# The gated unit's two products as 2x2 blocks: seven block products for eight

## The chip, the cores and the metric

The kernel runs on one core of a Trainium2 chip. The time is the device time of one execution in microseconds (us). TensorE multiplies matrices, VectorE and ScalarE work element by element and may read and write PSUM, GpSimd works on SBUF only, SyncE issues transfers.

## The reference

A linear attention feeds a router with eight experts (all float32), and its result x (1536 tokens, 384 features) a gated unit. The change concerns the last function:

```python
def _moe2_ref(x, w_gate, w_val, w_out) -> np.ndarray:
    g = x @ w_gate
    silu = g * (1.0 / (1.0 + np.exp(-g)))
    val = x @ w_val
    return (silu * val @ w_out).astype(np.float32)
```

w_gate and w_val are 384 x 1536, w_out is 1536 x 384, all three given as float64.

## The kernel before

The stages follow one another: attention and routing, experts, gated unit. A number is split in a high half (a rounded copy, made by ScalarE) and a low half (the rest, by VectorE or GpSimd: "lowered"), and each product is three matmuls: high x high, high x low, low x high.

**Gated unit.** The 1536 hidden features are six chunks c of 256, each two f of 128; the 384 input features are three k blocks of 128; the tokens are four groups g of 384 (TG). For a chunk and a group, `inner` sums gate and value over k in two PSUM banks for each f, 36 matmuls of 384 columns in all; ScalarE takes the Silu (L1095), VectorE multiplies (L1096), ScalarE rounds (L1099), GpSimd lowers (L1100). `outer` multiplies by w_out, three tiles of 128 tokens a group (L1111 to L1113, six matmuls a tile and chunk), and adds to `acc` (L1118 for the first chunk, L1120 later). Chunks 0 to 2 run chunk by chunk. For chunks 3 to 5 the group is the outer loop, and a tile sums all three chunks in PSUM; then it is stored by an indirect DMA from GpSimd's queue (L1122).

**Conversion.** `convert_all` turns the float64 weights into halves: 18 items (gate, value and output weights of each chunk), 768 columns each. An item's steps: Square on ScalarE and L811 on VectorE; L817; L823; L830 (all VectorE); the high half (ScalarE, L837); the low half (L842, on VectorE during the experts and on GpSimd in the gated unit). A new item starts every five calls of `background`, which stand by hand between the other work. 15 calls stand in the experts stage; chunks 0 and 1 have buffers there (`mp`), a third buffer comes with the gated unit.

**Experts.** Eight experts of 16 steps f (eight up, eight down). Each expert's own weights are split by ScalarE (L732) and VectorE (L733). The last expert also splits the tokens of groups 0 and 1 (`x2_split`).

On every engine the order of the code is the order of work. PSUM has eight banks: three for `pa_tile`, and in the gated unit two for `pg2` and three for `ps_o`.

Of the kernel before, what the change touches and what calls it, by code (L numbers as in the profile page):

```python
# [23 lines left out]
P = 128  # L24
# [36 lines left out]
FF_WEIGHTS = {"w_gate": [P, KD, 256], "w_val": [P, KD, 256], "w_out": [P, 2, DM]}  # L61
# [8 lines left out]
class Kernel:  # L70
# [14 lines left out]
    def run(self):  # L85
        tc, nc = self.tc, self.nc
        with ExitStack() as top, tc.manual_schedule():
# [7 lines left out]
            with ExitStack() as ex:  # L95
# [9 lines left out]
                self.x2s = [[mp.tile([P, KD, TG], F32R, name=f"x2{q}{g}") for q in "hl"] for g in range(2)]  # L105
                self.wff = [self.weights_ff(mp, i) for i in range(2)]
# [656 lines left out]
    def convert_all(self):  # L763

        items = [(m, c) for c in range(NC) for m in FF_WEIGHTS]

        def load(i):
            if i < len(items):
                m, c = items[i]
                raw = self.mp.tile([P, 2 * UC], I32, name="raw64", tag="raw64", bufs=2)  # L770
                self.nc.sync.dma_start(out=raw, in_=self.a[m][c].bitcast(I32))
                return raw, self.convert(lambda: self.wff[c % 3][m])
# [3 lines left out]
        for n in range(5 * len(items) + 1):  # L776
            if n % 5 == 0:
                cur[n // 5 + 1] = load(n // 5 + 1)
            for i in (n // 5 - 1, n // 5):
                j = n - 5 * i  # L780
                if 0 <= i < len(items) and j < 6:
                    raw, steps = cur[i]
                    steps[j](raw)
# [10 lines left out]
    def weights_ff(self, pool, i):  # L794

        return {
            m: [pool.tile(shape, F32R, name=f"{m}_{q}{i}") for q in ("hi", "lo")] for m, shape in FF_WEIGHTS.items()
        }

    def convert(self, outs):  # L800
# [4 lines left out]
        word = lambda raw, i: raw.rearrange("p (c two) -> p c two", two=2)[:, :, i]  # L805

        def s0(raw):
            t["mag"] = self.mp.tile([P, cols], F32, name="mag", tag="mag", bufs=2)
            nc.scalar.activation(t["mag"], word(raw, 1).bitcast(F32), AF.Square)
            t["bits"] = self.mp.tile([P, cols], I32, name="bits", tag="bits", bufs=2)  # L810
# [17 lines left out]
        def s3(raw):  # L828
# [3 lines left out]
            )  # L832

        def s4(raw):
            hi_out = outs()[0]
            t["m3"] = t["mag"].rearrange("p (a b) -> p a b", a=hi_out.shape[1])
            nc.scalar.copy(hi_out, t["m3"])  # L837

        def s5(raw):
            hi_out, lo_out = outs()  # L840

            (nc.vector if self.in_experts else nc.gpsimd).tensor_sub(lo_out, t["m3"], hi_out.bitcast(F32))  # L842

        return [s0, s1, s2, s3, s4, s5]


# [101 lines left out]
    def experts(self, st):  # L948
# [53 lines left out]
        last, xrs = None, {}  # L1002
        for e in range(E):
            hc, py = self.tiles()
            for f in range(2 * NF):
# [8 lines left out]
                if f == (5 if e == 0 else 1):  # L1014
# [8 lines left out]
                    if e == 0:  # L1023
                        self.background(1, 2)
# [13 lines left out]
                if f in ((12, 14) if 0 < e < E - 3 else (10, 12, 14) if 0 < e < E - 1 else ()):  # L1038
                    self.background(1, 2)
# [6 lines left out]
                if e == E - 1 and NF <= f < NF + 2 * KD:  # L1046
                    self.x2_split((f - NF) // KD, [(f - NF) % KD])
# [8 lines left out]
    def x2_split(self, g, ks):  # L1056
        nc = self.nc
        xh, xl = self.x2s[g]
        src = self.x2[:, :, g * TG:(g + 1) * TG]
        for k in ks:  # L1060
            nc.scalar.copy(xh[:, k], src[:, k])
            nc.vector.tensor_sub(xl[:, k], src[:, k], xh[:, k].bitcast(F32))

    def gated(self, st, at_end=lambda: None):
        nc, a = self.nc, self.a
        NG, NTT = N // TG, TG // P
        wk = self.pool(st, "wk", side="right")
        pg2 = self.pool(st, "pg2", 2, space=PSUM)
        ps_o = self.pool(st, "ps_o", 3, space=PSUM)
        self.wff.append(self.weights_ff(wk, 2))  # L1070
        self.x2s += [[wk.tile([P, KD, TG], F32R, name=f"x2{q}{g}") for q in "hl"] for g in range(2, NG)]
# [3 lines left out]
        acc = wk.tile([P, NT, DM], F32, name="acc")  # L1075
        later = []

        def inner(c, g, steps, limit):

            parts = []  # L1080
            xh, xl = self.x2s[g]
            for f in range(2):
                pg = {}
                if later:
                    self.x2_split(*later.pop(0))
                fs = slice(f * P, (f + 1) * P)
                for m in ("w_gate", "w_val"):
                    wh, wl = self.wff[c % 3][m]
                    pg[m] = (pg2.tile([P, 512], F32, name="g2", tag="g2") if f else self.pa_tile())[:, 0:TG]
                    for k in range(KD):  # L1090
                        nc.tensor.matmul(pg[m], lhsT=wh[:, k, fs], rhs=xh[:, k], start=(k == 0), stop=False)
                        nc.tensor.matmul(pg[m], lhsT=wh[:, k, fs], rhs=xl[:, k], start=False, stop=False)
                        nc.tensor.matmul(pg[m], lhsT=wl[:, k, fs], rhs=xh[:, k], start=False, stop=(k == KD - 1))  # L1093
                sg = wk.tile([P, TG], F32, name="sg", tag="sg", bufs=3)
                nc.scalar.activation(sg, pg["w_gate"], AF.Silu)  # L1095
                nc.vector.tensor_mul(sg, pg["w_val"], sg)  # L1096
                h_ = wk.tile([P, TG], F32R, name="ah", tag="ah", bufs=8)
                l_ = wk.tile([P, TG], F32R, name="al", tag="al", bufs=8)
                nc.scalar.copy(h_, sg)  # L1099
                nc.gpsimd.tensor_sub(l_, sg, h_.bitcast(F32))  # L1100
                parts.append((h_, l_))
                self.background(steps, *limit)
            return [(c, f, *parts[f]) for f in range(2)]
# [194 lines left out]
```

## Time and profile before

| | us |
|---|---|
| three runs | 442.28, 443.30, 443.99 (median 443.3) |
| profiled execution | 444.58 |
| its span, first to last instruction | 442.9 |
| TensorE, matmuls | 428.2 busy, 97% |
| VectorE | 288.1 busy, 65% |
| ScalarE | 213.4 busy, 48% |
| GpSimd | 155.8 busy, 35% |

The span is counted from the first to the last instruction of the profiled execution; the time includes what lies around it. In profile rows PE is TensorE's matmuls, PEld its weight loads, DVE VectorE, ACT ScalarE, POOL GpSimd.

### The profile page before, as it was taken

The numbers are of one execution on the slowest core, as the hardware profiler recorded it, in microseconds if no ns is written. First come the engines' busy times: TensorE is split into PE (matmuls) and PEld (weight loads), VectorE is DVE, ScalarE is ACT, GpSimd is POOL, SyncE is SP. The second block draws the span as 40 slices with busy tenths as digits, with TensorE's granted clock in tenths as the row PEclk, the third lists the DMA queues.
The fourth block names the chain that finished last, engine by engine and source line by source line (L and its number), as shares of the span: only waits on it lengthen the run. The fifth ranks groups of instructions, "written<-read, shape, count | busy, mean of one in ns | idle before, by whom it ended". The sixth has DMA issues, their size and how long they took to land. (4 is left out here: it accounts for less than half of the span.)

```text
span 442.9 us, 8350 instructions
## 1 busy us (share of the span) xinstructions
PE 428.2 (97%) x3180; PEld 415.7 (94%) x3180; DVE 288.1 (65%) x559; ACT 213.4 (48%) x470; POOL 155.8 (35%) x147
## 2 busy tenths in 40 slices
PE   8889999999999999999999999999999999999991
PEld 7778889999999999999999999999999999999991
DVE  6979996867887888895685879988774121212120
ACT  2677784656666666665465533444252121220310
POOL 5845653101120110000444546463565323232331
PEclk9989999999999999999999999999999999999997
DMA  7998952699999999602023242324200100001001
GB/s 259 356 304 274 360 226 89 195 362 304 347 222 219 294 253 228 230 1 73 0 80 122 86 142 73 123 92 142 74 0 1 53 1 22 32 0 56 1 21 41
DMA packets 24817, 63.78 MB, mean 144 GB/s; under 512 B 4800, under 2 KB 10048, under 8 KB 24768
## 3 DMA queue, kind: packets, MB, share of 16 engines
q1 hardware_dynamic: 22128, 57.43, 41.7%
q0 software_dynamic: 1920, 4.73, 2.9%
q10 hardware_dynamic: 720, 1.00, 0.8%
q8 instruction: 27, 0.44, 0.4%
q14 instruction: 22, 0.18, 0.1%
HBM read 55.67 MB, written 7.48 MB: 143 GB/s over the span
## 5 line engine op out<-in xcount | busy, mean ns | idle before, releaser
L1100 POOL TENSOR_TENSOR al<-sg,ah 128x384 fp32r<-128x384 f32 x48 | 54.5, 1135 | 128.2 <-ACT ah L1099 128.2
L733 DVE TENSOR_TENSOR wlo<-raw,whi 128x768 fp32r<-128x768 f32 x60 | 57.3, 956 | 9.7 <-ACT whi L732 8.8
L1099 ACT CAST ah<-sg 128x384 fp32r<-128x384 f32 x48 | 24.7, 515 | 78.0 <-DVE sg L1096 78.0
L865 PE MATMUL py<-hc,whi 128*128 128x448 f32 x192 | 62.2, 378 | 0.0
L876 PE MATMUL A<-xc,whi 128*128 128x224 f32 x336 | 56.7, 274 | 0.0
L866 PE MATMUL py<-hc,wlo 128*128 128x224 f32 x192 | 51.4, 268 | 0.0
L876 PEld LDWEIGHTS A<-xc,whi 128*128 128x128 f32 x336 | 51.0, 192 | 0.1
L732 ACT CAST whi<-raw 128x768 fp32r<-128x768 f32 x60 | 49.8, 837 | 1.3 <-PE py L865 0.7
L1111 PE MATMUL po<-w_out_hi,ah 128*128 128x384 f32 x144 | 48.6, 337 | 0.0
L1113 PE MATMUL po<-w_out_hi,al 128*128 128x384 f32 x144 | 48.5, 337 | 0.0
L1112 PE MATMUL po<-w_out_lo,ah 128*128 128x384 f32 x144 | 48.5, 337 | 0.0
L876 PE MATMUL A<-xc,wlo 128*128 128x224 f32 x168 | 46.1, 275 | 0.0
L943 POOL DMA_INDIRECT ids<-tok,by_expert x12 | 13.6, 1133 | 79.0 <-DMA ids<-tok,by_expert 71.1
L1120 DVE TENSOR_TENSOR acc<-acc,po 128x384 f32<-128x384 f32 x36 | 19.3, 546 | 30.9 <-PE po L1113 30.9
L865 PEld LDWEIGHTS py<-hc,whi 128*128 128x128 f32 x192 | 36.3, 189 | 2.7
L866 PEld LDWEIGHTS py<-hc,wlo 128*128 128x128 f32 x192 | 36.7, 191 | 0.0
L1096 DVE TENSOR_TENSOR sg<-g,sg 128x384 f32<-128x384 f32 x24 | 13.3, 555 | 35.8 <-PE g L1093 31.1
L1096 DVE TENSOR_TENSOR sg<-A,sg 128x384 f32<-128x384 f32 x24 | 13.3, 554 | 35.5 <-PE A L1093 31.8
L895 ACT ACTIVATE hc<-A 128x224 fp32r<-128x224 f32 x64 | 23.2, 362 | 21.2 <-PE A L876 18.4
L278 ACT ACTIVATE AT<-ident,c 128x128 f32<-128x128 f32 x96 | 29.4, 389 | 8.2 <-DVE c L265 8.2
L876 PEld LDWEIGHTS A<-xc,wlo 128*128 128x128 f32 x168 | 32.3, 192 | 0.0
L1095 ACT ACTIVATE sg<-A 128x384 f32<-128x384 f32 x24 | 11.7, 486 | 34.1 <-PE A L1093 34.1
(177 smaller groups left out, 1096.9 us busy)
## 6 DMA issues: line engine op xcount, KB each, us to landing
raw<-in_w SPq DMA_DIRECT2D x62, 384.0 KB, 7.6
rkT<-in_rkT SPq DMA_DIRECT2D x12, 512.0 KB, 5.6
rk<-in_rk SPq DMA_DIRECT2D x12, 384.0 KB, 5.6
raw<-in_w_gate SPq DMA_DIRECT2D x6, 768.0 KB, 4.2
raw<-in_w_val SPq DMA_DIRECT2D x6, 768.0 KB, 4.4
raw<-in_w_out SPq DMA_DIRECT2D x6, 768.0 KB, 4.5
x_disp<-zero SPq DMA_DIRECT2D x8, 336.0 KB, 7.6
xr<-x_disp SPq DMA_DIRECT2D x8, 336.0 KB, 6.5
```

The costliest lines, as they stand in the source:

```text
L278: nc.scalar.activation(AT[i][:, j, hp], ident, AF.Copy, scale=cc[i][:, j, hp:hp + 1])
L732: nc.scalar.copy(h_, raw)
L733: nc.vector.tensor_sub(l_, raw, h_.bitcast(F32))
L865: nc.tensor.matmul(ps[:, 0:2 * BLK], lhsT=wh, rhs=xc, start=first, stop=False, skip_group_check=True)
L866: nc.tensor.matmul(ps[:, HI], lhsT=wl, rhs=xc[:, HI], start=False, stop=last, skip_group_check=True)
L876: self.nc.tensor.matmul(ph[:, HI], lhsT=w[:, k, fs], rhs=x[1][:, k, half], start=(k == 0 and i == 0), stop=(k == KD - 1 and i == 2),)
L1096: nc.vector.tensor_mul(sg, pg["w_val"], sg)
L1099: nc.scalar.copy(h_, sg)
L1100: nc.gpsimd.tensor_sub(l_, sg, h_.bitcast(F32))
L1111: nc.tensor.matmul(po, lhsT=ah[:, ts_], rhs=wh, start=(i == 0), stop=False)
L1112: nc.tensor.matmul(po, lhsT=ah[:, ts_], rhs=wl, start=False, stop=False)
L1113: nc.tensor.matmul(po, lhsT=al[:, ts_], rhs=wh, start=False, stop=(i == len(parts) - 1))
```

## The change

Two groups of tokens make a pair p, x1 and x2. Over the k blocks 0 and 1, [gate; value] times [x1, x2] is a 2x2 by 2x2 block product, and seven products take the place of eight, at the price of sums: four of weights (S1 to S4, two VectorE operations in each of the value's steps s4 and s5, then a high and a low half of 1024 columns), four of tokens (T1 to T4, in `x_pair`: four steps for each pair, eight in all), and some of results. The k block 2 keeps its four plain products. A `block` is a chunk, a pair and one f.

Banks are now `pb` (from `pa_tile`), and `pa`, `pc`, `pd` of their own: `pb` collects gate x x11, is copied to `pa` by ScalarE, goes on to collect; `pc` and `pd` are written by VectorE as `pb + m5`, and products are added on top of all three. Two matmuls at the start open the banks that are written by other engines. `ps_o` has two banks.

The output tiles (`sum_tile`, six matmuls) stand between the products; all six chunks are now added into `acc` by VectorE (the first is copied by ScalarE as before). The weights have two buffers, and only chunk 0's in the experts stage; 19 calls of `background` stand there instead of 15, always three in experts 1 to 6. In a block three to six calls are placed (four in the steady chunks, none in the first two blocks, which run the token sums of pair 1). The Silu table is loaded in the last expert. The value of `gate0` is multiplied at the end of a block, and its halves are taken at the start of the next.

```diff
+GATE, VAL1, VAL2, S1, S2, S3, S4 = 0, 3, 4, 5, 6, 7, 8
+X11, X21, X31, X22, X32, T1, T2, T3, T4 = range(9)
+NW, NX = 9, 9
...
-                self.x2s = [[mp.tile([P, KD, TG], F32R, name=f"x2{q}{g}") for q in "hl"] for g in range(2)]
-                self.wff = [self.weights_ff(mp, i) for i in range(2)]
+                self.xb = [self.x_rooms(mp, 0)]
+                self.wff = [self.weights_ff(mp, 0)]
...
+        shapes = {"in": [P, NW, 256], "out": [P, 2, DM]}
+        return {m: [pool.tile(shape, F32R, name=f"w{m}_{q}{i}") for q in ("hi", "lo")] for m, shape in shapes.items()}
...
+            self.gate_m3 = t
+            return [s0, s1, s2, s3, lambda raw: high(t["m3"], GATE, KD), lambda raw: low(t["m3"], GATE, KD)]
...
+            high(t["m3"][:, 1:3], VAL1, 2)
+            g, v = gate["m3"], t["m3"]
+            sums = t["sums"] = self.comb(256)
+            nc.vector.tensor_sub(sums[:, 2], g[:, 0], v[:, 0])
+            nc.vector.tensor_add(sums[:, 0], v[:, 0], v[:, 1])
...
+            low(t["m3"][:, 1:3], VAL1, 2)
+            g, sums = gate["m3"], t["sums"]
+            nc.vector.tensor_sub(sums[:, 1], sums[:, 0], g[:, 0])
+            nc.vector.tensor_sub(sums[:, 3], g[:, 1], sums[:, 1])
+        return [s0, s1, s2, s3, s4, s5, lambda raw: high(t["sums"], S1, 4), lambda raw: low(t["sums"], S1, 4)]
...
+        prep = self.x_pair(0)
...
-                        self.background(1, 2)
+                        self.background(1, 1)
...
-                if f in ((12, 14) if 0 < e < E - 3 else (10, 12, 14) if 0 < e < E - 1 else ()):
-                    self.background(1, 2)
+                if f in ((10, 12, 14) if 0 < e < E - 1 else ()):
+                    self.background(1, 1)
...
-                if e == E - 1 and NF <= f < NF + 2 * KD:
-                    self.x2_split((f - NF) // KD, [(f - NF) % KD])
+                if e == E - 1 and f == NF:
+                    nc.scalar.activation(self.ep.tile([P, 1], F32, name="silu"), self.zero[:, 0:1], AF.Silu)
+                if e == E - 1 and f >= NF - 2 and prep:
+                    prep.pop(0)()
...
+        def high(at, src, n):
+            nc.scalar.copy(xh[:, at:at + n], src)
+        def low(at, src, n, eng=nc.vector):
+            eng.tensor_sub(xl[:, at:at + n], src, xh[:, at:at + n].bitcast(F32))
...
+            t["t"] = self.comb(TG)
+            high(X11, x1, 3)
+            nc.vector.tensor_sub(t["t"][:, 0], x2[:, 0], x1[:, 0])
+            nc.vector.tensor_sub(t["t"][:, 1], x2[:, 1], t["t"][:, 0])
+            low(X11, x1, 3, plain)
+        def step1():
+            high(X22, x2[:, 1:3], 2)
+            nc.vector.tensor_sub(t["t"][:, 2], x2[:, 1], x2[:, 0])
+            nc.vector.tensor_sub(t["t"][:, 3], x1[:, 1], t["t"][:, 1])
+            low(X22, x2[:, 1:3], 2, plain)
...
+            high(T1, t["t"][:, 0:2], 2)
+            low(T1, t["t"][:, 0:2], 2)
+        def step3():
+            high(T3, t["t"][:, 2:4], 2)
+            low(T3, t["t"][:, 2:4], 2)
...
+        ps_o = self.pool(st, "ps_o", 2, space=PSUM)
+        pg2 = self.pool(st, "pg2", space=PSUM)
+        pc, pa, pd = (pg2.tile([P, 512], F32, name=n)[:, 0:TG] for n in ("gc", "ga", "gd"))
...
+        STEPS = {(0, 0, 0): (-1, -1, 0), (0, 0, 1): (-1, -1, 0), (0, 1, 0): (2, 2, 2), (0, 1, 1): (2, 2, 2)}
...
+            if c == 0:
+                nc.scalar.copy(acc[:, n], po)
+            else:
+                nc.vector.tensor_add(acc[:, n], acc[:, n], po)
...
+        def halves(sg, eng=nc.gpsimd):
...
+            limit = (c + 2, True) if p else (c + 1, False)
+            last = (c, p, f) == (NC - 1, 1, 1)
+            room = lambda name: wk.tile([P, TG], F32, name=name, tag=name, bufs=2)
...
+            opened(pa)
+            pb = self.pa_tile()[:, 0:TG]
+            product(pb, GATE, X11, True)
+            nc.scalar.copy(pa, pb)
+            later = bool(before)
+            if before:
+                before.pop()()
+            if tiles:
+                sum_tile()
+            product(pd, S1, T1, True)
+            m5 = room("m5")
+            nc.scalar.copy(m5, pd)
+            if later:
+                side(steps[2])
+            opened(pc)
+            product(pb, S2, T2)
+            nc.vector.tensor_add(pc, pb, m5)
+            add_tiles()
+            side(steps[0])
+            product(pa, GATE + 1, X21)
+            product(pa, GATE + 2, X31)
+            gate0 = room("gate0")
+            nc.scalar.activation(gate0, pa, AF.Silu)
+            sum_tile()
+            product(pb, S3, T3)
+            nc.vector.tensor_add(pd, pb, m5)
+            add_tiles()
+            side(steps[1])
+            product(pc, S4, X22)
+            product(pc, GATE + 2, X32)
+            gate1 = room("gate1")
+            nc.scalar.activation(gate1, pc, AF.Silu)
+            sum_tile()
+            if last:
+                add_tiles()
+                sum_tile()
+            product(pd, VAL2, X32)
+            nc.vector.tensor_mul(gate1, pd, gate1)
+            add_tiles()
+            low_eng = nc.vector if last else nc.gpsimd
+            parts = [None, halves(gate1, low_eng)]
+            product(pb, VAL1, T4)
+            product(pb, VAL2, X31)
+            nc.vector.tensor_mul(gate0, pb, gate0)
+            def rest():
+                parts[0] = halves(gate0, low_eng)
+            before.append(rest)
+            return parts
...
+                blocks = [block(c, p, f, STEPS.get((c, p, f), (1, 1, 2)), c > 0 or p > 0 and f > 0) for f in range(2)]
...
+                for j in (1, 0):
+                    sums += [(c, (2 * p + j) * NTT + tt, [(f, blocks[f], j) for f in range(2)]) for tt in range(NTT)]
+        before.pop()()
+        while sums:
+            if len(sums) == 1:
+                at_end()
+            sum_tile()
+            add_tiles()
```

## Rows read from the trace of the kernel before

**Rows 1.** Page, part 1: engine, busy us, share of span, instructions.
```profile
PE 428.2 (97%) x3180; PEld 415.7 (94%) x3180; DVE 288.1 (65%) x559; ACT 213.4 (48%) x470; POOL 155.8 (35%) x147
```

**Rows 2.** Stretches: us; busy of five engines (instructions); clock, DMA share, GB/s.
```profile
162.00:177.00 15.00, 15.00 (x118) 14.63 (x117) 12.72 (x23) 10.32 (x22) 0.96 (x1) 1.00 1.00 251
177.00:192.00 15.00, 15.00 (x118) 14.63 (x117) 13.49 (x25) 9.81 (x22) 0.00 (x0) 1.00 0.51 171
...
240.00:300.00 60.00, 60.00 (x346) 60.00 (x345) 51.10 (x57) 25.93 (x46) 32.45 (x20) 1.00 0.33 106
300.00:340.00 40.00, 40.00 (x231) 40.00 (x230) 29.85 (x41) 16.53 (x29) 21.69 (x15) 1.00 0.18 60
340.00:400.00 60.00, 60.00 (x346) 60.00 (x345) 10.62 (x20) 12.58 (x25) 19.75 (x21) 1.00 0.06 20
```

**Rows 3.** Timeline, both ends of the gated stage: start, us, engine, line.
```profile
207.48 0.35 PE L1091 MATMUL A<-x2h,w_gate_hi 128*128 128x384 f32 x1
...
433.21 0.34 PE L1113 MATMUL po<-w_out_hi,al 128*128 128x384 f32 x1
433.59 0.55 DVE L1120 TENSOR_TENSOR acc<-acc,po 128x384 f32<-128x384 f32 x1 [2.60 <-PE po L1113]
434.42 0.96 POOL L1122 DMA_INDIRECT out<-acc,idx  x1 [2.19 <-POOLq L115]
```

**Rows 4.** Single lines: engine, operation, count; ns shortest/median/longest; first, last start.
```profile
L1091 PE MATMUL A<-x2h,w_gate_hi x72: 334/336/350, 207.5 to 418.7; 128*128 128x384 f32 x72
...
L1096 DVE TENSOR_TENSOR sg<-A,sg x24: 543/556/559, 210.9 to 421.1; 128x384 f32<-128x384 f32 x24
...
L1099 ACT CAST ah<-sg x48: 512/514/520, 211.5 to 424.8; 128x384 fp32r<-128x384 f32 x48
...
L1100 POOL TENSOR_TENSOR al<-sg,ah x48: 1007/1022/1731, 212.1 to 425.4; 128x384 fp32r<-128x384 f32 x48
...
L1118 ACT COPY acc<-po x12: 469/476/491, 222.0 to 252.1; 128x384 f32<-128x384 f32 x12
...
L1120 DVE TENSOR_TENSOR acc<-acc,po x36: 537/542/555, 259.7 to 433.6; 128x384 f32<-128x384 f32 x36
...
L1122 POOL DMA_INDIRECT out<-acc,idx x12: 958/961/987, 343.4 to 434.4; - x12
...
L811 DVE TENSOR_SCALAR bits<-raw x15: 543/548/1382, 214.5 to 329.3; 128x768 int32<-128x768 int32 x15
...
L817 DVE SCALAR_TENSOR_TENSOR bits<-raw,bits x15: 941/1234/2492, 218.8 to 331.1; 128x768 int32<-128x768 int32 x15
...
L842 POOL TENSOR_TENSOR w_gate_lo<-mag,w_gate_hi x5: 1852/2062/2172, 225.0 to 322.7; 128x768 fp32r<-128x768 f32 x5
...
L1062 DVE TENSOR_TENSOR x2l<-x,x2h x6: 550/552/558, 200.9 to 203.2; 128x384 fp32r<-128x384 f32 x6
...
L297 DVE COPY_PREDICATED AT<-mask,A x24: 710/725/741, 12.7 to 64.8; 128x512 f32<-128x512 uint8 x24
```

**Rows 5.** Timeline, VectorE and GpSimd while a chunk is converted.
```profile
280.58 1.02 POOL L1100 TENSOR_TENSOR al<-sg,ah 128x384 fp32r<-128x384 f32 x1 [1.97 <-ACT ah L1099]
...
280.75 1.68 DVE L817 SCALAR_TENSOR_TENSOR bits<-raw,bits 128x768 int32<-128x768 int32 x1
...
281.57 2.55 POOL L842 TENSOR_TENSOR w_val_lo<-mag,w_val_hi 128x768 fp32r<-128x768 f32 x1
...
282.34 0.54 DVE L1120 TENSOR_TENSOR acc<-acc,po 128x384 f32<-128x384 f32 x1
...
282.81 2.13 DVE L823 SCALAR_TENSOR_TENSOR bits<-raw,bits 128x768 int32<-128x768 int32 x1
```

**Rows 6.** Stretches of the attention stage, columns as in the second group.
```profile
16.00:20.00 4.00, 3.29 (x46) 2.72 (x42) 3.38 (x7) 2.76 (x9) 2.90 (x3) 1.00 0.90 315
...
24.00:28.00 4.00, 2.33 (x36) 2.13 (x36) 3.68 (x8) 4.00 (x15) 1.47 (x2) 0.86 1.00 350
28.00:32.00 4.00, 4.00 (x43) 3.15 (x39) 1.79 (x4) 1.93 (x7) 2.43 (x3) 0.71 0.87 300
```

More of the change, by code (lines that the diff above doesn't have):

```diff
@@ L763, in convert_all @@
     def convert_all(self):
-        items = [(m, c) for c in range(NC) for m in FF_WEIGHTS]
+        items = [(m, c) for c in range(NC) for m in FF_ITEMS]
         def load(i):
@@ L780, in convert_all @@
                 j = n - 5 * i
-                if 0 <= i < len(items) and j < 6:
+                if 0 <= i < len(items) and j < len(cur[i][1]):
                     raw, steps = cur[i]
@@ L805, in convert @@
         word = lambda raw, i: raw.rearrange("p (c two) -> p c two", two=2)[:, :, i]
+        wide = lambda: self.wff[c % 2]["in" if m != "w_out" else "out"]
         def s0(raw):
@@ L1074, in gated @@
         idx = wk.tile([P, NT], I32, name="idx2")
[L1075 to L1103, printed above, removed]
@@ L1129, in gated @@
[L1129 to L1150 removed]
+        acc = self.x2.rearrange("p k n -> p (k n)")[:, 0:NT * DM].rearrange("p (t d) -> p t d", d=DM)
@@ new lines, in gated, with tile_of @@
+        sums, todo = [], []
+        STEPS = {(0, 0, 0): (-1, -1, 0), (0, 0, 1): (-1, -1, 0), (0, 1, 0): (2, 2, 2), (0, 1, 1): (2, 2, 2)}
+        def tile_of(c, n, parts):
+            po = ps_o.tile([P, DM], F32, name="po", tag="po")
+            ts_ = slice(n % NTT * P, (n % NTT + 1) * P)
+            for i, (f, halves_, j) in enumerate(parts):
+                ah, al = halves_[j]
+                wh, wl = (w[:, f] for w in self.wff[c % 2]["out"])
+                nc.tensor.matmul(po, lhsT=ah[:, ts_], rhs=wh, start=(i == 0), stop=False)
+                nc.tensor.matmul(po, lhsT=ah[:, ts_], rhs=wl, start=False, stop=False)
+                nc.tensor.matmul(po, lhsT=al[:, ts_], rhs=wh, start=False, stop=(i == len(parts) - 1))
+            return lambda: added(c, n, po)
@@ new lines, in gated @@
+        prep, before = self.x_pair(1), []
+        for c in range(NC):
+            for p in range(2):
+                blocks = [block(c, p, f, STEPS.get((c, p, f), (1, 1, 2)), c > 0 or p > 0 and f > 0) for f in range(2)]
+                if c == 1 and p == 1:
+                    nc.vector.tensor_copy(idx, idx_f)
+                for j in (1, 0):
[6 more added lines that the diff above has]
+            add_tiles()
```

134 lines of the change are left out of this document (65 added, 69 removed).

## The prediction

> **What bounds the kernel now.** I read the page's first part, then the busy time by stretch, the timeline at both ends of the gated stage, the lines of that stage, and one stretch in which VectorE and GpSimd share it. TensorE is busy for 97% of the span [rows 1]. From expert 5 to 400 us it is full in every stretch, at a granted clock of 1.00 [rows 2]. A full row could hide pauses, because each matmul is recorded at 0.336 us [rows 4] while the next one starts earlier. So I take the pace from the ends: the first gated matmul starts at 207.48, the last at 433.21 [rows 3], and between them lie 1296 (twelve groups of 72 for gate and value, one of which is shown, and three of 144 for the output). 225.73 / 1295 = 0.1743 us each. Nothing else in the stage ends last: VectorE is at 85% while weights are converted (51.10 of 60) and at 18% afterwards [rows 2]. After the last matmul come one addition and one indirect store (433.59 and 434.42, 0.96 us) [rows 3]; the span closes at 442.9, the profiled execution at 444.58.
>
> **The matmuls.** Before, a chunk, a pair of token groups and an f take 2 x 2 x 3 = 12 block products of three matmuls. Now the first two k blocks take seven products, the third still four: 11. That is 3 matmuls fewer in each of 6 x 2 x 2 = 24 blocks, 72 in all, each with its weight load: 72 x 0.1743 = 12.55 us. The output keeps 432. Two opening matmuls come in, 0.35 us. If nothing waits: 444.58 - 12.55 + 0.35 = 432.4.
>
> **What comes in for it.** In a steady block TensorE now issues 33 + 18 = 51 matmuls, 8.89 us. VectorE has the two additions into PSUM (pc and pd), two multiplications, three additions into acc, and about four steps of conversion. No row shows VectorE writing PSUM. The nearest is L1096, same width, one operand from PSUM: 0.556 us [rows 4]; L297, 512 wide, takes 0.725, the upper bound. I take 0.556, as for the multiplications. Additions into acc take 0.542. A chunk's conversion is three items of one L811 (0.55) and three operations like L817 (0.94 undisturbed), 10.1 us, and four new sums of 256 columns, some 0.4 each by L1062's 0.552 for 384: 11.7 a chunk, 2.9 a block. Together 4 x 0.556 + 3 x 0.542 + 2.9 = 6.8 of 8.89 us. ScalarE has two PSUM copies (0.476, as L1118), two Silu, two casts (0.514) and its part of the conversion, some 4.5 us: room enough. So no engine is overfull; what counts is lateness, since TensorE now comes back to the same bank within a block. pb is read by ScalarE, then by VectorE for pc, then for pd, each before its next product.
>
> **VectorE and GpSimd take turns.** In [rows 5] L817, queued behind GpSimd's L1100 that ends at 281.60, ends 0.83 later; L842, queued behind L817, ends 1.69 after it; L823, queued behind L842, ends 0.82 after that. L1120, which reads PSUM, runs through the middle of L842 in 0.54. So the additions to pc and pd don't wait for GpSimd, but the conversion queued ahead of them does. Successive VectorE records overlap by 0.08 us.
>
> **A steady block, from its first matmul.** A result is out about 0.27 us after its issue slot (last start 433.21, addition 433.59, less the slot of 0.17, gives 0.21; I add a margin). The previous block's pd is finished six matmuls before its end, so gate1 is multiplied by -0.2, cast (0.514) by 0.35 and lowered on GpSimd (1.02) by 1.43. Its last product is multiplied from 0.27 to 0.83. A conversion operation waits for GpSimd and ends at 2.25; GpSimd lowers gate0 until 3.13; the second operation ends at 3.95; pc is added by 4.43. TensorE needs it after 27 matmuls, at 4.70: 0.2 us to spare. pd comes after S3T3 (30 matmuls, 5.5 with the delay) and is done by about 6.6 even behind a lowering of 768 columns; TensorE needs it after 42, at 7.32. ScalarE's copy into pa is done at 1.27, needed at 12 x 0.1743 = 2.09. So an ordinary block waits for nothing.
>
> The blocks that carry the value's sums are later: two to four small operations more, and a lowering of 512 columns (about 1.15) between them. In chunks 1 to 4 (16 blocks of four steps, 15 steps to a chunk, so that the phase moves) I find three in which pc comes 0.7, 1.0 and 1.2 us late, and little else: 2.8 us. Behind the late addition stand the additions into acc and the next conversion, for which TensorE doesn't wait, with two ps_o banks; on ScalarE one Square a chunk waits for sums that read the buffer it will write, and holds a Silu that nothing needs for 2 us. If the second operation before pc always meets a long lowering, as L817's longest row (2.49) did, pc is 0.8 late in each of 16 blocks: 13 us. Chunk 5 converts nothing: no wait. From below the cost is nothing, as the margins are positive.
>
> **The first chunk.** The first three blocks have no output tile between the first product and ScalarE's copy: 0.1, 0.4 and 0.3 us. The token sums of the second pair stand in the first two blocks; their GpSimd lowerings (1152 and 768 columns, some 2.7 and 1.9 us by L842's shortest, 1.85 for 768) hold VectorE's small sums, which push the multiplication on pd by 0.5. Then two blocks carry twelve steps of the second chunk, six each: VectorE falls behind by about 1.6 in the second and 0.7 in the block after. Together 3.7 us; from below about 1 (the bare copies), from above 6, if both six-step blocks wait as the second does.
>
> **The experts' side.** 19 steps instead of 15, so one more in experts 1 to 4 (0.94 us in 16), and the token sums of pair 0 in the last expert: some 6 us of VectorE (four sums of 0.55, lowerings of 1152 and three times 768 columns) for 3.3. The cover is the row of expert 6 (177 to 192): with three steps an expert already, VectorE 13.49 of 15 and TensorE full [rows 2]. Two weight loads come an expert earlier and a third is added in expert 6, on SP's queue ahead of the expert's loads; DMA is at 1.00 in expert 5 but 0.51 in expert 6. I cost this at nothing; without that cover it would be the four steps and the 2.7, 6.5 us. The Silu table load moves into the last expert; before it delayed nothing on TensorE either.
>
> **The end.** The last six tiles follow at 6 matmuls each, 1.05 us, and each needs an indirect store of 0.96 on GpSimd plus its issue (I estimate 0.14, half of what lies between the addition's end at 434.14 and the store at 434.42): it lags by some 0.05 a tile, 0.3 us. That the last halves move to VectorE keeps GpSimd free for it.
>
> **Sum.** 432.4 + 2.8 + 3.7 + 0.3 = 439.2 for an execution that took 444.58. The median before is 443.3, 1.3 lower; so 438.0.
>
> **The rivals.** *Every wait is hidden* (the phases fall better than my walk, and TensorE's queue covers the first chunk): 432.4 to 433.4, less 1.3: 431 to 432. For it: the margins are positive in 13 of 16 blocks. Against: 0.2 us is thin. *VectorE sets the pace*: the addition to pc comes 0.8 late in all sixteen blocks: 439.2 + 10.2 - 1.3 = 448. It turns slower than before once the waits together pass 12.2 us, and is seen as such past 14.4. For it: VectorE was at 85% in this stage, with L817 at 1.23 median against 0.94. Against: that was up to seven steps to 54 matmuls, now four to 51. Halfway, with twice my waits, it gives 443. *The experts fall behind*: 438 + 6.5 = 444.5; against it stands the row of expert 6.
>
> *The clock falls*: short pauses in every block bring the lower level back. Between 24 and 32 us TensorE was busy for 2.33 of 4 us and the clock granted then and in the next 4 us was 0.86 and 0.71 [rows 6], that is partly at 1.2 instead of 2.4 GHz. Those 8 us lost some 1.7; one such dip in each of five chunks would give 438 + 8.6 = 446.6. Against: at 16 to 20 us TensorE was busy for 3.29 of 4 and kept 1.00 [rows 6], and the pauses that I forecast are shorter than that one. The Trainium skill (TensorE: Matmul & The Clock Gate, A second HAM failure mode: psum-queue depth-cycling) says that cycling through PSUM banks with short idle spells between groups made the clock swing and cost throughput; by that rule this rival would be the forecast, and the trace bears it out only after the long pause. *The change doesn't do what it says* would need a matmul pace that grows with the mixed order; steps between gate products and output tiles already run at 0.17, so I give it nothing.
>
> **Chances.** My forecast, 434 to 441: 0.50. All hidden, about 431.5: 0.22. VectorE behind: 0.18, half of it near 443 and half at 445.5 or above. Experts: 0.05, near 444.5. Clock: 0.05, near 446.6. A difference under 0.5% (2.2 us) can't be told from none here. So faster 0.72, same 0.09 + 0.05 = 0.14, slower 0.09 + 0.05 = 0.14. The range leaves out the lower half of what is hidden best and the two slow ends: 431.0 to 445.5; the forecast's own is 434 to 441.
>
> **What would show it.** Right: 792 and 432 matmuls at 0.174, and TensorE's idle time put down to VectorE at the product on S3T3, some 7 us in the gated stage, most of it between 207 and 245 us and none after chunk 4's conversion; the experts ending at 207.4. Wrong: a pace other than 0.174, a clock below 1.00, TensorE waiting for ScalarE in steady blocks, idle time before 207, or a pause in every block.

## The result and the profile after

The change made the kernel slower: median 448.0 us (six runs, 446.44 to 451.65) against 442.69 (six runs), ratio 1.0125 with a 95% interval of 1.0099 to 1.015. The prediction was 438.0, faster, with a range from 431.0 to 445.5. The profiled execution of the changed kernel took 446.44, its span 444.6.

In the page's first part TensorE's matmuls fell by 70, as counted, but VectorE rose from 65% to 80% [rows 1]:

```profile
PE 420.4 (95%) x3110; PEld 402.2 (90%) x3110; DVE 357.0 (80%) x661; ACT 240.3 (54%) x521; POOL 168.6 (38%) x151
```

The same stage by stretches, columns as in [rows 2]:

```profile
240.00:280.00 40.00, 39.13 (x222) 38.49 (x221) 32.73 (x44) 23.30 (x46) 22.79 (x15) 1.00 0.20 73
280.00:320.00 40.00, 38.31 (x218) 37.55 (x217) 37.28 (x48) 17.64 (x33) 18.39 (x13) 1.00 0.21 68
320.00:360.00 40.00, 38.78 (x219) 38.14 (x218) 35.79 (x49) 18.50 (x35) 19.52 (x13) 1.00 0.21 71
360.00:400.00 40.00, 39.67 (x225) 39.03 (x225) 27.37 (x42) 15.77 (x31) 16.20 (x12) 1.00 0.00 1
```

TensorE has holes now, and VectorE is busy for up to 37.28 of 40 us. The clock is 1.00 in all of them. Both ends of the gated stage, in the timeline [rows 3]:

```profile
206.41 0.34 PE L1203 MATMUL ga<-xbh,win_hi 128*128 128x384 f32 x1
...
433.47 0.96 POOL L1162 DMA_INDIRECT out<-x,idx  x1 [0.30 <-issue]
433.61 0.34 PE L1153 MATMUL po<-wout_hi,al 128*128 128x384 f32 x1
433.98 0.55 DVE L1160 TENSOR_TENSOR x<-x,po 128x384 f32<-128x384 f32 x1 [0.50 <-PE po L1153]
434.73 0.96 POOL L1162 DMA_INDIRECT out<-x,idx  x1 [0.30 <-DVE x L1160]
435.99 0.96 POOL L1162 DMA_INDIRECT out<-x,idx  x1 [0.30 <-issue]
```

227.20 us hold 1226 matmuls. At 0.1743 they would take 213.5, so TensorE waits for 13.7 us in this stage; the prediction had 6.5. Where they lie follows from the distance between successive copies into `pa` (L1210, one a block) less the matmuls issued between them at 0.1743 each (34 in block 0 with the second opening one, 33, 45, then 51). Below, blocks are numbered from 0, four to a chunk; a chunk, pair and f is written (c, p, f).

| us waited | predicted | measured |
|---|---|---|
| blocks 0 to 2, first chunk | 1.3 | 2.90 + 0.38 + 0.73 = 4.01 |
| blocks 3 to 5 (six steps; after it) | 2.3 | 3.37 - 0.33 - 0.22 = 2.82 |
| blocks 6 to 19 | 2.8 | 5.48, of it 2.20 in block 10 (2,1,0), 1.82 in 14, 0.83 in 18 |
| blocks 20 to 23, last tiles | 0 | 1.4 |
| experts | 0 | 1.1 |
| last matmul to the end of the span | 0.3 more | 10.99 against 9.7, 1.3 more |

The profiled execution of before had lost 2.15 in attention [rows 6], which this one had not (first token transposes of the experts at 90.18 and 88.03), so the like of it for comparison is 444.58 - 2.15 = 442.4. Then 442.4 - 12.2 (70 matmuls) + 13.7 + 1.1 + 1.3 = 446.3, and 446.44 was measured. The median is another 1.6 higher; that part is likely the clock, treated below.

The view of waits, TensorE's in the gated stage (us in total, times, longest):

```profile
PE A L1198 <- DVE gc L1223: 3.5, 4, 1.3
PE gd L1198 <- DVE gd L1232: 3.0, 4, 1.9
PE gd L1198 <- DVE gate L1244: 0.9, 2, 0.7
PE po L1151 <- DVE x L1160: 0.6, 1, 0.6
```

Every line names VectorE: the additions to pc (L1223) and pd (L1232), the multiplication that the next block's pd waits for (L1244), and one addition into `acc`. The view counts idle time from the end of a 0.336 us record, so each wait costs some 0.26 more in the pace: the two of block 10 below, 0.93 and 0.76, cost 2.20. The operations themselves are as short as predicted:

```profile
L1223 DVE TENSOR_TENSOR gc<-A,m x24: 551/560/567, 208.7 to 419.3; 128x384 f32<-128x384 f32 x24
...
L1232 DVE TENSOR_TENSOR gd<-A,m x24: 550/556/567, 212.6 to 421.9; 128x384 f32<-128x384 f32 x24
...
L1210 ACT COPY ga<-A x24: 463/463/474, 207.3 to 417.2; 128x384 f32<-128x384 f32 x24
```

So they are late, not long. The timeline shows what they stand behind, first in block 0, then in block 10:

```profile
209.18 0.55 DVE L1107 TENSOR_TENSOR comb<-x 128x384 f32<-128x384 f32 x1
...
209.44 2.79 POOL L1100 TENSOR_TENSOR xbl<-x,xbh 128x1152 fp32r<-128x1152 f32 x1 [44.87 <-ACT xbh L1097]
...
209.76 2.89 DVE L1108 TENSOR_TENSOR comb<-x,comb 128x384 f32<-128x384 f32 x1
...
212.19 2.13 POOL L1100 TENSOR_TENSOR xbl<-x,xbh 128x768 fp32r<-128x768 f32 x1
...
212.57 0.55 DVE L1232 TENSOR_TENSOR gd<-A,m 128x384 f32<-128x384 f32 x1
...
213.18 0.44 PE L1198 MATMUL gd<-xbh,win_hi 128*128 128x384 f32 x1 [1.94 <-DVE gd L1232]
...
300.60 0.55 DVE L1223 TENSOR_TENSOR gc<-A,m 128x384 f32<-128x384 f32 x1
...
301.10 2.39 POOL L852 TENSOR_TENSOR win_lo<-comb,win_hi 128x1024 fp32r<-128x1024 f32 x1 [0.84 <-ACT win_hi L848]
...
301.20 0.44 PE L1198 MATMUL A<-xbh,win_hi 128*128 128x384 f32 x1 [0.93 <-DVE gc L1223]
...
301.53 2.78 DVE L829 SCALAR_TENSOR_TENSOR bits<-raw,bits 128x768 int32<-128x768 int32 x1
...
304.23 0.55 DVE L1232 TENSOR_TENSOR gd<-A,m 128x384 f32<-128x384 f32 x1
...
304.84 0.44 PE L1198 MATMUL gd<-xbh,win_hi 128*128 128x384 f32 x1 [0.76 <-DVE gd L1232]
```

In both places GpSimd starts a lowering as soon as ScalarE's high half is there (the row's releaser). A token sum of 0.55 us, started 0.32 after a lowering of 2.79, takes 2.89 and ends 0.42 after it; a conversion step, started 0.43 after a lowering of 2.39, takes 2.78 and ends 0.82 after the lowering does. The addition to pd stands in VectorE's queue behind it and TensorE behind the addition. The addition itself, with one operand in PSUM, runs in 0.55 beside the second lowering (2.13, from 212.19). The Trainium skill (SBUF — State Buffer, Who interferes with whom) has the same: "Issue order, not op shape, decides who blocks." These rows agree: both VectorE operations that were stretched, to 2.89 and 2.78 us, started after the lowering.

### The profile page after: what moved, and what is told of

Its sections match the earlier page's. It is cut to its first block, busy times and chain, and to the rows that moved or that the text cites. A ratio compares the mean times of both kernels' runs of the same rounds, so it can differ in the third digit from the quotient of the medians.

```text
span 444.6 us, 8390 instructions
## 1 busy us (share of the span) xinstructions
PE 420.4 (95%) x3110; PEld 402.2 (90%) x3110; DVE 357.0 (80%) x661; ACT 240.3 (54%) x521; POOL 168.6 (38%) x151
## 5 line engine op out<-in xcount | busy, mean ns | idle before, releaser
L1179 POOL TENSOR_TENSOR al<-gate,ah 128x384 fp32r<-128x384 f32 x46 | 52.7, 1150 | 93.8 <-ACT ah L1178 93.6
L1151 PE MATMUL po<-wout_hi,ah 128*128 128x384 f32 x144 | 48.7, 338 | 0.6 <-DVE x L1160 0.6
L1153 PE MATMUL po<-wout_hi,al 128*128 128x384 f32 x144 | 48.8, 339 | 0.0
L1152 PE MATMUL po<-wout_lo,ah 128*128 128x384 f32 x144 | 48.5, 337 | 0.0
L1178 ACT CAST ah<-gate 128x384 fp32r<-128x384 f32 x48 | 24.7, 515 | 42.2 <-DVE gate L1244 41.1
L1198 PE MATMUL A<-xbh,win_hi 128*128 128x384 f32 x120 | 41.4, 345 | 3.8 <-DVE gc L1223 3.5
L973 POOL DMA_INDIRECT ids<-tok,by_expert x12 | 13.9, 1158 | 74.8 <-DMA ids<-tok,by_expert 66.8
L1198 PE MATMUL A<-xbh,win_lo 128*128 128x384 f32 x120 | 40.4, 337 | 0.0
L1198 PE MATMUL A<-xbl,win_hi 128*128 128x384 f32 x120 | 40.4, 336 | 0.0
L1160 DVE TENSOR_TENSOR x<-x,po 128x384 f32<-128x384 f32 x60 | 32.4, 542 | 3.5 <-PE po L1153 3.5
```

The source lines that it names most:

```text
L1151: nc.tensor.matmul(po, lhsT=ah[:, ts_], rhs=wh, start=(i == 0), stop=False)
L1152: nc.tensor.matmul(po, lhsT=ah[:, ts_], rhs=wl, start=False, stop=False)
L1153: nc.tensor.matmul(po, lhsT=al[:, ts_], rhs=wh, start=False, stop=(i == len(parts) - 1))
L1160: nc.vector.tensor_add(acc[:, n], acc[:, n], po)
L1179: eng.tensor_sub(l_, sg, h_.bitcast(F32))
L1198: nc.tensor.matmul(ps, lhsT=w, rhs=x, start=first and i == 0, stop=False, skip_group_check=True)
```

## The experiments

The waits of each profiled execution, in us, worked out as above; the end is the span from the last matmul:

| run | blocks 0–1 | 2–5 | 6–11 | 12–15 | 16–19 | gated stage | experts | end |
|---|---|---|---|---|---|---|---|---|
| the changed kernel | 3.27 | 3.56 | 2.51 | 2.05 | 0.92 | 13.68 | 1.08 | 10.99 |
| e1_same | 3.29 | 3.58 | 2.53 | 2.04 | 0.94 | 13.75 | 1.09 | 10.90 |
| e2_no_conversion | 4.02 | 0.41 | 0.03 | 0.06 | 0.05 | 5.65 | 1.09 | 12.59 |
| e3_weight_sums_gpsimd | 3.28 | 4.84 | 2.68 | 0.31 | 0.41 | 12.93 | 8.21 | 12.97 |
| e4_token_sums_vector | 1.83 | 3.56 | 2.54 | 2.04 | 0.92 | 12.25 | 1.09 | 10.72 |
| e5_late_halves | 4.50 | 3.92 | 2.03 | 0.93 | 0.38 | 13.15 | 1.07 | 13.11 |
| e6_low_half_later | 4.32 | 3.54 | 2.52 | 2.02 | 0.52 | 14.32 | 1.82 | 10.50 |
| e7_lowerings_vector | 3.28 | 4.57 | 3.02 | 2.39 | 1.85 | 16.48 | 1.08 | 12.91 |
| e8_all_four | 2.27 | 1.81 | 1.90 | 0.95 | 1.20 | 9.52 | 2.16 | 10.66 |
| e9_spread | 3.29 | 4.48 | 0.36 | 0.48 | 1.24 | 11.23 | 1.09 | 10.59 |
| e10_spread_tokens_experts | 1.05 | 2.96 | 0.36 | 0.48 | 1.25 | 7.47 | 0.96 | 10.54 |
| e11_and_late_halves | 1.09 | 3.54 | 0.52 | 0.31 | 1.26 | 8.09 | 0.96 | 10.84 |
| e12_third_square_buffer | 1.05 | 2.94 | 0.39 | 0.51 | 1.13 | 7.41 | 0.83 | 11.26 |

**e1_same.** The changed kernel once more, no edit.

> The changed kernel as it is, for the spread of its runs beside their granted clocks. In its profile TensorE's matmuls of the gated stage take 227.4 us where 1226 at 0.1743 would take 213.7, and the six runs lie between 446.4 and 451.7. If VectorE's lateness alone makes it slower, the waits repeat at the same places and all runs lie within some 1 us of 447. If the clock has a part, the longer runs show the lower mean clock: a run at 0.981 should be some 3 to 5 us longer than one at 0.992.

446.84 us, ratio 1.0117 (1.006 to 1.0174). The waits repeat to 0.03 us in each group of blocks: they are set by the order of work, not by chance, and a difference of some tenths in the table can be read, except in blocks 0 and 1 of e2, e5 and e6, where the clock fell (below). The clock has a part in the times: the run at 0.981 took 451.1 us, that at 0.992 took 445.77.

**e2_no_conversion.** All six chunks use the weights of chunk 0; the conversion of chunks 1 to 5 is left out, with its loads.

```diff
-                self.background(n, *limit)
+                pass
...
-                wh, wl = (w[:, wi, fs] for w in self.wff[c % 2]["in"])
+                wh, wl = (w[:, wi, fs] for w in self.wff[0]["in"])
```

> Leaves out the conversion of chunks 1 to 5 in the gated stage, with its loads; every chunk uses the weights of chunk 0. If the conversion ahead of the additions to pc and pd makes them late, the waits of the blocks (0,1,0), (0,1,1), (2,1,0), (3,1,0) and (4,1,0), 9 us by the profile (0.7, 3.4, 2.2, 1.8, 0.8), go, the first two blocks keep their 3.1, and the time is about 438 (447 less 9). If the handing of banks between engines is the cost, VectorE's write into PSUM among it, the waits stay, though their places may change: 445 or more. If the saving of 72 matmuls were not real, the time would not come under the kernel before, 442.7.

439.71 us, ratio 0.994 (0.9918 to 0.9961). From block 3 on nothing waits, though TensorE, the banks and the additions to pc and pd are as in the changed kernel. What is left of the waits view is the first block and the last tiles:

```profile
PE gd L1197 <- DVE gd L1231: 1.9, 1, 1.9
PE po L1150 <- DVE x L1159: 0.6, 1, 0.6
```

So the exchange of seven products for eight is worth what was counted, and the conversion, on whichever engine, is what takes most of it back. The time did not fall by all of the 8 us: in this execution the end was 1.6 us longer (so it was in e3, e5 and e7), and the first block held a lower clock.

**e3_weight_sums_gpsimd.** The four weight sums on GpSimd, in s4 and s5:

```diff
-            nc.vector.tensor_sub(sums[:, 2], g[:, 0], v[:, 0])
+            nc.gpsimd.tensor_sub(sums[:, 2], g[:, 0], v[:, 0])
```

and likewise the other three.

> The four sums of weights of each chunk on GpSimd instead of VectorE, also in the experts stage. If these sums, which stand ahead of the additions to pc and find GpSimd's lowerings between them, make the late blocks late, the waits of 3.4, 2.2, 1.8 and 0.8 us fall by half or more, and the 1 us that expert 5 lost goes: 447 - 5 = 442. If VectorE is simply full, the relief is its four times 0.42 us a chunk: 447 - 2 = 445. If GpSimd's longer sums hold VectorE's other operations up as much as they relieve it, no change: 447.

454.96 us, ratio 1.0285 (1.0263 to 1.0308). The waits of blocks 12 to 19 nearly vanish (2.97 to 0.72), those of 2 to 5 grow, and the experts lose 7 us more, most of it in one wait in expert 4, on ScalarE's token halves:

```profile
PE A L906 <- ACT xc L754: 5.5, 1, 5.5
```

The sums matter where they stand ahead of pc, but GpSimd is no place to put them: in the experts they stand in its queue behind a scatter of indices (L973, until 159.28) and end at 162.31, the next item's Square waits for them until 162.34, and the token halves (L754) stand behind the Square on ScalarE. After that pause the clock is 0.50 from 164 to 168 us. For the theory that the sums alone are the cause it speaks neither clearly for nor against.

**e4_token_sums_vector.** The token sums of pair 1 in five steps, all their low halves on VectorE, three steps in block 1:

```diff
-            low(X11, x1, 3, plain)
...
-            low(X22, x2[:, 1:3], 2, plain)
...
+            low(X11, x1, 3)
...
-... (0, 0, 1): (-1, -1, 0), ...
+... (0, 0, 1): (-1, -1, -1), ...
```

> The token sums of the second pair in five steps instead of four, with all lowerings on VectorE and none on GpSimd, and each lowering after the sums. In the profile of the changed kernel the second token sum waited 2.4 us for GpSimd's lowerings (1152 and 768 columns, 4.9 us) and the addition to pd behind it came 1.9 late. If that lock is the cause of the first two blocks' 3.1 us, they lose under 1.2 and the time is about 445; if VectorE has too much to do there, it gets worse, by its 2.3 us more of lowering: 447 to 449.

445.0 us, ratio 1.0058 (1.0028 to 1.0088). Block 0 goes from 2.90 to 0.17, block 1 from 0.38 to 1.65, and nothing else moves. That shows the cause of the first block's pause: GpSimd's lowerings beside the small sums. The two blocks together keep 1.83, more than the 1.2 expected, since block 1 now carries the lowerings. The ratio fell by 0.0059 from e1's, some 2.6 us, though the waits fell by only 1.5 in the profiled execution; the clock (below) is the likely rest.

**e5_late_halves.** The previous block's second pair of halves is taken after the addition to pc, so that GpSimd's lowering of it starts later:

```diff
-            if before:
-                before.pop()()
...
             nc.vector.tensor_add(pc, pb, m5)
+            if before:
+                before.pop()()
```

> The halves of the previous block's gate0 are taken after the addition to pc instead of before it, so that GpSimd's lowering of gate0 no longer lies between the two steps of conversion that stand ahead of that addition. Same work. If the taking of turns with GpSimd makes the addition late, the waits of the blocks (0,1,1), (2,1,0), (3,1,0) and (4,1,0), 3.4, 2.2, 1.8 and 0.8 us, lose some 0.9 each, the length of one such lowering: 446.8 - 3.5 = 443.3. If the number of VectorE operations alone decides, nothing changes: 446.8.

447.43 us, ratio 1.0103 (1.0044 to 1.0163): no gain. The three late blocks are relieved as the theory of turns says (2.20 to 0.79, 1.82 to 1.40, 0.83 to 0.31), and new waits come up in blocks 7 (1.47) and 9 (0.34). This execution also had a lower clock after the first block's pause, which is the likely source of the 1.2 us more in blocks 0 and 1:

```profile
210.00:212.00 2.00, 0.97 (x6) 0.65 (x4) 2.00 (x1) 1.15 (x2) 2.00 (x2) 1.00 0.00 0
212.00:214.00 2.00, 1.08 (x5) 1.09 (x6) 2.00 (x3) 0.00 (x0) 2.00 (x1) 0.93 0.00 0
214.00:216.00 2.00, 2.00 (x8) 2.00 (x8) 1.87 (x4) 0.51 (x1) 0.07 (x1) 0.50 0.00 0
216.00:218.00 2.00, 2.00 (x10) 1.84 (x9) 0.11 (x2) 1.06 (x3) 1.00 (x1) 0.71 0.00 0
```

**e6_low_half_later.** The value's low half moves from s5 to s6, behind the sums:

```diff
-            low(t["m3"][:, 1:3], VAL1, 2)
...
+        def s6(raw):
+            high(t["sums"], S1, 4)
+            low(t["m3"][:, 1:3], VAL1, 2)
```

> The low half of the value's weights (512 columns, on GpSimd) is taken one step later, with the high half of the sums, so that it no longer lies between the four sums. Same work. In the profile of the changed kernel, block (2,1,0) had it from 298.79 to 300.26, and VectorE's next operation waited for it. If that turn is the cause, the waits of the late blocks lose up to 1.2 us in (0,1,1) and (2,1,0): about 444.5; if the sums themselves are, nothing changes: 446.8.

447.98 us, ratio 1.0115 (1.0047 to 1.0184): a miss. Only block 18 gained, 0.4, and the experts lost 0.7 more; blocks 0 and 1 took 1.0 more at a lower clock. Where that one lowering stands did not matter to blocks 3, 10 and 14.

**e7_lowerings_vector.** All converted low halves on VectorE, so that only the 384-column lowerings of the hidden values stay on GpSimd:

```diff
-            (nc.vector if self.in_experts else nc.gpsimd).tensor_sub(lo, src, hi.bitcast(F32))
+            nc.vector.tensor_sub(lo, src, hi.bitcast(F32))
```

> The low halves of all converted weights are taken by VectorE, in the gated stage too; GpSimd keeps only the halves of the gated values. That is 3072 columns more a chunk on VectorE, some 3.4 us of the 35.8 that a chunk has, so about 90% of it is full, and 8 us a chunk less on GpSimd. If what counts is the taking of turns, the late blocks get better by more than the load makes the others worse: 444 or less. If it is the load of VectorE, waits appear in most blocks and the time grows to 450 or more.

454.01 us, ratio 1.0254 (1.0188 to 1.0319). The long turns are gone, and VectorE is busy for less of the stretch than before the edit (35.26 against 37.28 of 40, GpSimd 9.81 against 18.39):

```profile
280.00:320.00 40.00, 38.85 (x221) 38.21 (x220) 35.26 (x55) 17.58 (x33) 9.81 (x8) 1.00 0.18 64
```

Yet the waits over the whole stage grow by 2.8 us, in every group but the first blocks (of the 7.6 us between the profiled executions the end, 1.9 longer, is another part, and 3.0 lie in attention, which the edit doesn't touch: the first token transposes come at 91.01 against 88.03, at a clock of 0.95 and 0.62 between 24 and 32 us). So the turns with GpSimd are one way to be late and not the cause itself: whatever fills VectorE's queue ahead of the addition makes it late, blocked time or work.

**e8_all_four.** e4, e5 and e6 together, and the experts' calls placed otherwise:

```diff
-                if f in ((10, 12, 14) if 0 < e < E - 1 else ()):
+                if f in ((12, 14) if e == 4 else (10, 12, 14) if 0 < e < E - 1 else (4,) if e else ()):
```

> Together: halves of gate0 later, low half of the value's weights later, the token sums lowered on VectorE in five steps, and in the experts stage one step of conversion moved from expert 4 to expert 7. If the gains are where the profile puts the waits they add up: 3.5 + 2.3 + 1.9 and the 1.0 of expert 5, from 446.8 to about 438, under the kernel before (442.7). If a queue that is relieved in one place is late in the next, less than half of it comes: 443 or more.

443.45 us (ten runs), ratio 1.0014 (0.9982 to 1.0045): no longer slower than before, but less than half of the 8.7 us that the gains would add up to came. The waits of the stage are down to 9.52, and the experts lose 2.16: 1.37 from expert 4 to expert 5, where e6's part of the edit alone had 1.74, 0.60 from expert 5 to 6, and 0.14 behind.

**e9_spread.** Two conversion steps stood between a block's start and the addition to pc. One of them now stands at the block's end, behind the multiplication of `gate1` and ahead of the last two pb products; the work is the same.

```diff
-STEPS.get((c, p, f), (1, 1, 2))
+STEPS.get((c, p, f), (1, 1, 1, 1))
...
             parts = [None, halves(gate1, low_eng)]
+            side(steps[3])
```

> One of the two steps of conversion that stand ahead of the addition to pc goes to the end of the block before, behind the multiplication of gate1 and ahead of that of gate0, for which TensorE doesn't wait: four places with one step each. Same work. If lateness in VectorE's queue makes the waits, the place decides: those of the late blocks in chunks 1 to 4 (2.2, 1.8, 0.8) shrink to under 1.5 together, and the time is about 443.5 (446.8 less 3.3). If VectorE has too much to do in any order, they move elsewhere: 446 or more.

444.03 us (ten runs), ratio 1.0024 (0.9997 to 1.005). Block 10 goes from 2.20 to -0.01, block 14 from 1.82 to 0.61, block 18 from 0.84 to -0.18. A new one appears in block 17 (1.91), and block 4 goes from -0.34 to 0.92. This is the test that isolates the order: nothing leaves VectorE's queue and nothing moves between engines, and 2.5 us of waits go.

**e10_spread_tokens_experts.** e9, with the token sums in six steps on VectorE, as in e4, and the experts' calls of expert 4 and the last one moved:

```diff
-        STEPS = {(0, 0, 0): (-1, -1, 0), (0, 0, 1): (-1, -1, 0), ...
+        STEPS = {(0, 0, 0): (-1, -1, 0, -1), (0, 0, 1): (-1, -1, -1, 0), ...
...
-                if f in ((10, 12, 14) if 0 < e < E - 1 else ()):
+                if f in ((8, 12) if e == 4 else (10, 12, 14) if 0 < e < E - 1 else (4,) if e else ()):
```

> The spread steps, and the token sums lowered on VectorE in six steps of which none has more than one lowering, and in the experts stage expert 4 with two steps, both early in its down products, and expert 7 with one. By the theory of lateness the first two blocks keep under 1 us of their 3.1, the experts' 1.0 goes, and the chunks lose 3: 440, under the kernel before (442.7). If less than half of that comes, 443.5 or more.

440.44 us (ten runs), ratio 0.994 (0.9911 to 0.9968): faster than the kernel before by 0.6%, and than the changed one (1.0125, 1.0117). The waits are 7.47, 1.05 of them in the first two blocks. The loss in the experts did not go: 0.61 of its 0.96 now lies between the transposes of experts 5 and 6, 0.15 between those of 4 and 5. The largest wait left outside the first chunk is block 17, where the timeline shows another chain:

```profile
364.63 1.12 DVE L872 TENSOR_TENSOR comb<-mag,comb 128x256 f32<-128x256 f32 x1
...
365.67 1.63 DVE L823 TENSOR_SCALAR bits<-raw 128x768 int32<-128x768 int32 x1
...
365.83 0.89 ACT L821 ACTIVATE mag<-raw 128x768 f32<-128x768 f32 x1 [1.49 <-DVE comb L872]
...
366.63 0.47 ACT L1212 COPY ga<-A 128x384 f32<-128x384 f32 x1
...
367.16 0.44 PE L1200 MATMUL A<-xbh,win_hi 128*128 128x384 f32 x1 [0.91 <-ACT ga L1212]
```

A weight sum on VectorE (L872) holds the next item's Square (L821), which writes into the buffer that the sum reads; the copy into `pa` stands behind the Square on ScalarE, and TensorE behind the copy. The prediction had seen this hold, ahead of a Silu that nothing needs; in this order of steps it stands ahead of the copy.

**e11_and_late_halves.** e10 with e5's edit as well.

> As the run before, and the halves of gate0 are taken after the addition to pc. With one step ahead of that addition instead of two, the lowering of gate0 has nothing to hold up before it, but meets the step behind it, ahead of the addition to pd. If the lowering's place ahead of pc still costs, 1 us less than the run before; if it only moves the turn, the same or up to 1 us more.

440.28 us (nine runs), ratio 0.9945 (0.9919 to 0.997): no difference to e10.

**e12_third_square_buffer.** e10 with a third buffer for the Square and one step moved from block 3 to block 1:

```diff
-            t["mag"] = self.mp.tile([P, cols], F32, name="mag", tag="mag", bufs=2)
+            t["mag"] = self.mp.tile([P, cols], F32, name="mag", tag="mag", bufs=3)
...
-        STEPS = {... (0, 0, 1): (-1, -1, -1, 0), ... (0, 1, 1): (2, 2, 1, 1)}
+        STEPS = {... (0, 0, 1): (-1, -1, -1, 1), ... (0, 1, 1): (2, 1, 1, 1)}
```

> As the run with spread steps, tokens and experts, with a third buffer for the squares of the conversion (so that ScalarE's Square of the output weights no longer waits until VectorE has read the gate's square for the sums), and one step of the second chunk moved from block (0,1,1) to the end of (0,0,1). In the profile of that run ScalarE was held at 365.8 and its copy into pa came 0.9 late. If that wait is the cause of the 1.9 us in block 17 and of part of the 3.2 in block 3, they fall to under 0.4 and about 2.2, and the time is about 438 (440.4 less 2.5). If VectorE's lateness is behind both, ScalarE is early but TensorE waits for the additions: 440.

440.84 us (twelve runs), ratio 0.9957 (0.9927 to 0.9987). Block 17 goes from 1.91 to 0.04, which shows that the buffer held it, and block 3, from which a step was moved as well, from 3.17 to 2.06. But block 2 waits 0.6 more and block 18 goes from -0.17 to 1.43: the sum is as before (7.41). The waits view now names VectorE there, the addition to pd in block 3 (2.1) and that to pc in block 18 (0.5): the buffer decided in which block VectorE's lateness came out.

## Why the prediction was wrong

**What held.** The pace: the 1226 matmuls run at 0.1743 wherever they don't wait. The gain of 72 matmuls: e2 is under the kernel before with 5.65 us of waits left. The durations: 0.556 for VectorE's write to PSUM, 0.463 for ScalarE's copy against 0.476. The form of the waits: VectorE, at the products behind pc and pd; ordinary blocks wait for nothing (14 of the 23 distances are within 0.12 us of the count), nothing after chunk 4 but the last tiles.

**The step that failed** is the size of VectorE's lateness: the terms 2.8 and 3.7, 6.5 us together (their parts add up to 2.9 and 3.6), measured 12.3 up to block 19 (and 13.7 with the last tiles). Three blocks were late in chunks 1 to 4, as walked, but by 2.20, 1.82 and 0.83 in place of 1.2, 1.0 and 0.7. The walk let GpSimd take its turn after the VectorE operation queued ahead of it. On the chip GpSimd follows ScalarE's high half and is there first: in block 10 the addition to pc was late as walked, but then the 1024-column lowering got ahead of the next conversion step, and pd came late too. In block 0 it took 2.90 where 0.1 and a part of 0.5 stood: the walk had the held sums push the multiplication on pd, but a sum of 0.55 that stands ahead of the addition to pd was held, by the first lowering alone, until 212.65. Block 3, with six steps, took 3.37 in place of 1.6. That the place in the queue decides is shown by e4 and e9, which move those operations.

**The experts** were costed at nothing, under the cover of expert 6's row. They lost 1.1: from the transposes of expert 4 to those of expert 5 it took 17.22 in place of 16.21. Beside the matmuls of before, all of it falls on two starts in the up products, which wait for VectorE's half of the relu (L926) and cost 0.55 and 0.46 in the pace:

```profile
160.35 0.38 DVE L926 SCALAR_TENSOR_TENSOR hc<-A,hc 128x224 fp32r<-128x224 f32 x1
...
160.78 0.48 PE L906 MATMUL A<-xc,whi 128*128 128x224 f32 x2 [0.28 <-DVE hc L926]
...
162.25 0.48 PE L906 MATMUL A<-xc,whi 128*128 128x224 f32 x2 [0.20 <-DVE hc L926]
```

L926 starts 8.36 us after the transposes; before, its like started 6.92 after them. The value's item now has eight steps while a new item starts every five calls, so that one call can run a step of two items: between two token operations there VectorE has 2.08 us of conversion, before it had 0.95. The row of expert 6 had single steps and was no cover for that. e6 and e3, which change these steps, made the same stretch 17.95 and 24.34; e10, which gives expert 4 one call fewer and earlier, made it 16.36. No run changed only that, so the cause is likely and not shown by itself.

**The end** was costed at 0.3 and took 1.3. The issue between two stores was estimated at 0.14 and is 0.30: the stores follow at 0.96 + 0.30 = 1.26 where tiles follow at 1.05, so they fall 0.21 behind with each tile, and the last one starts 2.38 us after the last matmul, before 1.21. No run tried another end.

**The clock** was a rival with 0.05 that came in part. In the profiled execution TensorE paused in the first block and kept 1.00:

```profile
210.00:212.00 2.00, 1.24 (x8) 0.92 (x6) 2.00 (x1) 1.41 (x3) 2.00 (x1) 1.00 0.00 0
212.00:214.00 2.00, 0.82 (x5) 0.82 (x6) 2.00 (x3) 0.00 (x0) 2.00 (x2) 1.00 0.00 0
214.00:216.00 2.00, 1.83 (x10) 1.51 (x9) 2.00 (x4) 0.29 (x1) 0.32 (x1) 1.00 0.00 0
```

In e5 the same pause was followed by the lower level: 0.50 at 214 to 216, all of it at 1.2 GHz; so it was in e2 (0.50) and e6 (0.55). Ten runs of the changed kernel (e1's among them) have a mean of 448.1 us at a mean granted clock of 0.988, between 445.77 at 0.992 and 451.65 at 0.981; before it is 443.0 at 0.992 in 24 runs. That is the likely source of the 1.6 between the profiled execution and the median. In this profile the clock stayed at 1.00 from 240 to 400 us. So the swing that the prediction weighed by the Trainium skill (TensorE: Matmul & The Clock Gate, A second HAM failure mode: psum-queue depth-cycling) did not come in every block.

The miss of 10.0 us adds up: 7.2 of waits, 1.1 in the experts, 1.0 at the end and 1.6 of clock, less 0.9, since the prediction took off 1.3 for the execution it started from and that had lost 2.15.

**The rivals.** "VectorE sets the pace" gave 448 and hit the time, but by another way: not 0.8 us in all sixteen blocks, but three late ones, the first chunk, the experts, the end and the clock, so that its number was met by luck. Its middle case, 443, is halfway to 448; twice the forecast's waits would be 438 + 6.5 = 444.5. It turned slower past 12.2 us of waits, as it said; 13.7 came. When only the order changes (e9), the waits are 11.23 and the ratio is 1.0024; with the token lowerings moved from GpSimd to VectorE and the experts' calls placed otherwise as well (e10) they are 7.47, and the kernel is 0.6% faster than before.

**What stays open.** Why the clock falls after the first pause in some executions only; why the end is 1.6 to 2 us longer in the profiles of e2, e3, e5 and e7 (all of it lies behind the start of the last store, from which the span runs on for 10.2 to 10.7 us there and for 8.1 to 8.9 in the others); whether the overlapping steps alone are what the experts lose.

## What to carry to other kernels

When an engine's result goes back into the running product, count not its load but what stands ahead of that result in its queue, and for each of those operations who else may hold what it needs: here VectorE at 85% was harmless as long as nobody waited for it within a block; at 82 to 93%, with TensorE waiting within the block, it cost most of 13.7 us. Walk two engines that share SBUF access by when each one's own input is ready, not in step with the other's queue. Before giving up such a change, move background steps behind the last deadline of the block: the same work in another order (e9) turned 1.2% slower into 0.2%, and with the token lowerings on the other engine as well (e10) into 0.6% faster.

## What was not expected of the hardware

The same pause of TensorE, about 2 us of 4 in the first block, left the clock at 1.00 in one execution and took it to 0.50 in another of the same instructions there. Consecutive indirect stores from GpSimd's queue are 1.26 us apart (0.96 and 0.30 of issue), also when their data has been there for some time: the last one starts at 435.99, the addition ahead of it ended at 434.53.
